# Chunked attention and two feed-forward networks: attention's steps placed one by one in the plan, a GpSimd subtraction cut into four

## The chip, the cores and the metric

The kernel runs on one core of one Trainium2 chip. The metric is the device time of one execution in microseconds. The engines work from queues of their own: TensorE (PE in the rows; PEld is its weight load), VectorE (DVE), ScalarE (ACT), GpSimd (POOL) and SyncE (SP), whose queue here only issues DMAs.

## The reference

Eight batches of eight heads with 576 positions of 64 features are cut into chunks of 64 positions, and each chunk attends to itself alone. The result, 4608 tokens of 512 features, goes through two feed-forward networks of width 2048.

```
scores = (q_c @ k_c^T) / 8;  scores -= max(scores)
attn   = exp(scores) / (sum(exp(scores)) + 1e-9)
x      = attn @ v_c                       # [4608, 512]
r = max(x @ w_in, 0);  y = (s * r*r + b) @ w_out
h = y @ w2_in;         out = (h * sigmoid(1.702 * h)) @ w2_out
```

## The kernel before

Tokens are worked on in nine blocks of 512 (j = 0 to 8). A product of fp32 accuracy is made of three TensorE matmuls, since every operand is kept as a high and a low part: low times high, high times high, high times low. The weights come as 64-bit floats and are decoded on the chip.

One product of the first network is `gemm_in(f, j, i)` (L511): 12 matmuls of 512 columns into a PSUM tile `h`. From it ScalarE makes `r` (ReLU, L531), VectorE `r = s * r * r` (L532), ScalarE the high part `gh` (L533) and VectorE the low part `gl` (L534). `gemm_out` (L579) then multiplies `gh` and `gl` with the second weights into four `acc` tiles (L594), also 12 matmuls. TensorE's order alternates the two, with `gemm_out` for index i two indices (`LAG`) behind `gemm_in`, so four products lie between the end of a product `h` and the first use of its `gh`. At the end of a block the `acc` tiles are copied out as `ost` (L602 on VectorE, L604 on ScalarE).

Attention of block j is done while the products of block j-1 run. A `Pair` (L236) is two heads of one block, four pairs to a block. Its generator `steps` (L301) is: `qt` and `kt` by two VectorE transposes of q and k (L272); 32 small score matmuls (L307); on VectorE the maximum (L316) and its subtraction (L317); the exponential on ScalarE (L322); on VectorE the sum (L324), 1e-9 (L325), the reciprocal (L326) and the product (L327) into `p`; `turn` (L276), eight VectorE transposes of 32 partitions by 256 columns (L281) into `pt`; `second` (L290), 32 small matmuls with v (L292); `split_x` (L297), the high and low parts of x. Blocks 0 and 1 use `EarlyPair`, whose transposes are TensorE's.

Beside this, from block 2 on, the second network's weights are decoded (`decode_second`, L175: a load into a `wst` tile, then L124 and L133 on ScalarE, L125, L128 and L134 on VectorE, L136 on GpSimd, and a DMA out from GpSimd's queue), and sums and differences of their quarters are made for a later stage of the Strassen kind (`sums`, L189). In `sums` everything is GpSimd's: four operations on 128 by 128 tiles (L198 to L201), a rounding to the high parts of seven such tiles at once (L203), the subtraction that leaves the low parts of the seven (L204, 896 columns), and two DMAs out (L209), the high parts first. The `wst` tiles are three: a decode holds one and a call of `sums` two.

After block 8 come `second_weights`, the first block of the second network, and the class `Halves`, which does the second network for pairs of blocks with seven products instead of eight.

The order is a plan written by hand. `at(t, f)` notes a function under a place t, `steps_at` notes the successive stretches of a generator, up to its next `yield`; at the end all notes are sorted by t and called, which traces the instructions. One unit of t is one product: `gemm_in` stands at 0.5 and `gemm_out` at 1.6 of every two units. The framework then sets the order of each engine's queue (`schedule_with_timeline_sim=True`): what was traced earlier has precedence among what its own time model takes to be ready. On the chip a queue is worked off in that order, and an instruction that waits holds what stands behind it. All short-lived tiles of [128, 512] (`qt`, `kt`, `p`, `pt`, `r`, `wm`, `wc`, `ost`) share ten places (`tmp`).

A pair is planned by these lines of `plan_attention` (L483), with o its base place; five notes for 13 stretches, so that four stretches (maximum to transposes) are traced together at o + 2:

```
at(o - 6.5, pr.load_qk)
at(o + 2.5, pr.load_v)
steps_at(((o - 2, 3), (o + 1, 1), (o + 2, 4), (o + 8, 1), (o + 8.5, 1)), pr.steps)
```

Of the kernel before, what the change touches and what calls it, by code (L numbers as in the profile page):

```python
# [8 lines left out]
F32 = mybir.dt.float32  # L9
F32R = mybir.dt.float32r  # L10
# [3 lines left out]
ALU = mybir.AluOpType  # L14
# [5 lines left out]
CH = 64  # L20
# [4 lines left out]


FIRST_STEPS = (0, 0.6, 0.8, 1.1, 1.8, 2.4, 2.7, 3.6, 3.9, 4.5)
LAG = 2
STAGED = 8
OPS = 4  # L30
# [16 lines left out]
def chunk_attention_two_ffn(ctx, tc, q, k, v, w1_in, w1_out, s, b, w2_in, w2_out, out):  # L47
# [6 lines left out]
    nc = tc.nc  # L54
# [49 lines left out]
    def tmp(name, dtype=F32):  # L104
        return tpool.tile([P, NB_MAX], dtype, tag="tmp", name=name)
# [38 lines left out]
    def staged():  # L144
        return stpool.tile([P, NB_MAX, 2], I32, tag="wst", name="wst")
# [43 lines left out]
    def sums(kind, i, z):  # L189

        q = staged().rearrange("p f z -> p (f z)").bitcast(F32).rearrange("p (t c) -> p t c", c=P)
        one, two = ((1, 2), (0, 3)) if kind == "wi" else ((1, 0), (2, 3))
        for t, (a, b) in ((i, one), (i + KF // 2, two)):
            for c, to in ((z, a), (2 + z, b)):
                nc.sync.dma_start(out=q[:, to, :], in_=w2_dram[kind][t][:, c * P:(c + 1) * P])
        yield
        a21, a11, a12, a22, s1, s2, s3, s4 = (q[:, t, :] for t in range(8))
        nc.gpsimd.tensor_tensor(out=s1, in0=a21, in1=a22, op=ALU.add)  # L198
        nc.gpsimd.tensor_tensor(out=s3, in0=a11, in1=a21, op=ALU.subtract)
        nc.gpsimd.tensor_tensor(out=s2, in0=s1, in1=a11, op=ALU.subtract)  # L200
        nc.gpsimd.tensor_tensor(out=s4, in0=a12, in1=s2, op=ALU.subtract)  # L201
        hi = staged().rearrange("p f z -> p (f z)").bitcast(F32R).rearrange("p (t c) -> p t c", c=P)[:, 0:7, :]
        nc.gpsimd.tensor_copy(out=hi, in_=q[:, 1:8, :])  # L203
        nc.gpsimd.tensor_tensor(  # L204
            out=q[:, 1:8, :].bitcast(F32R), in0=q[:, 1:8, :], in1=hi.bitcast(F32), op=ALU.subtract
        )
        to = wi_sums[i][:, :, z] if kind == "wi" else wo_sums[:, :, i, z]
        for part, src in enumerate((hi.bitcast(F32), q[:, 1:8, :])):
            nc.gpsimd.dma_start(out=to[:, :, part, :], in_=src)  # L209
# [15 lines left out]
    def quarters(nch):  # L225

        for i in range(nch // 2):
            for e in range(2):
                for h in range(2):
                    yield e, i, e * (nch // 2) + i, h, heads[h], heads[h ^ e]

    class Pair:  # L236
# [32 lines left out]
        def stage_qk(self):  # L269
            self.qt, self.kt = tmp("qt")[:, 0:self.n], tmp("kt")[:, 0:self.n]  # L270
            for t, src in ((self.qt, self.raw[0]), (self.kt, self.raw[1])):
                nc.vector.transpose(out=t.rearrange("p (u l) -> p u l", l=BK), in_=src)  # L272
            yield
            yield

        def turn(self, p):  # L276
            pt = tmp("pt")[:, 0:self.n].rearrange("p (c t) -> p c t", t=CH)
            for r in heads:
                for eq in range(2):
                    for ek in range(2):  # L280
                        nc.vector.transpose(  # L281
                            out=pt[r.start + ek * BK:r.start + (ek + 1) * BK, :, eq * BK:(eq + 1) * BK],
                            in_=p[r.start + eq * BK:r.start + (eq + 1) * BK, :, ek * BK:(ek + 1) * BK],
                        )
            return pt

        def room_scores(self):
            return left
# [12 lines left out]
        def steps(self):  # L301

            yield from self.stage_qk()
            yield
            ps = self.room_scores().rearrange("p e (c t) -> p e c t", t=CH)
            for e, i, c, h, r, other in quarters(self.nch):
                nc.tensor.matmul(  # L307
                    out=ps[other, e, i, :], lhsT=self.qt[r, c * CH:(c + 1) * CH], rhs=self.kt[r, c * CH:(c + 1) * CH],
                    start=True, stop=True,
                )  # L310
            yield
            mx = spool.tile([P, self.nch], F32, tag="mx", name="mx")
            sm = spool.tile([P, self.nch], F32, tag="sm", name="sm")
            p = tmp("p")[:, 0:self.n].rearrange("p (c t) -> p c t", t=CH)
            by_bank = mx.rearrange("p (e c) -> p e c", e=2)
            nc.vector.tensor_reduce(out=by_bank, in_=ps, axis=AX.X, op=ALU.max)  # L316
            nc.vector.tensor_tensor(  # L317
                out=p.rearrange("p (e c) t -> p e c t", e=2), in0=ps,
                in1=by_bank.unsqueeze(3).to_broadcast([P, 2, self.nch // 2, CH]), op=ALU.subtract,
            )  # L320
            yield
            nc.scalar.activation(out=p, in_=p, func=AF.Exp, scale=scale)  # L322
            yield
            nc.vector.tensor_reduce(out=sm, in_=p, axis=AX.X, op=ALU.add)  # L324
            nc.vector.tensor_scalar(out=sm, in0=sm, scalar1=1e-9, scalar2=None, op0=ALU.add)  # L325
            nc.vector.reciprocal(out=sm, in_=sm)  # L326
            nc.vector.tensor_tensor(  # L327
                out=p, in0=p, in1=sm.unsqueeze(2).to_broadcast([P, self.nch, CH]), op=ALU.mult
            )
            yield  # L330
            turned = self.turn(p)
            yield
            self.second(turned)
            yield
            self.split_x()
            done[0, self.j] = done.get((0, self.j), 0) + 1

    class EarlyPair(Pair):
# [21 lines left out]
        def turn(self, p):  # L360
            ps = acc_ps.tile([P, self.n], F32, tag=f"acc{2 * (self.hp % 2)}", name="pT")
            for i in range(self.n // P):
                nc.tensor.transpose(
                    ps[:, i * P:(i + 1) * P], p[:, 2 * i:2 * i + 2, :].rearrange("p c t -> p (c t)"), ident
                )
            pt = tmp("pt")[:, 0:self.n]
            nc.vector.tensor_copy(out=pt, in_=ps)
            return pt.rearrange("p (c h q) -> p c h q", h=2, q=CH)


        def room_scores(self):
# [92 lines left out]
    def at(t, f, *a):  # L464
        ITEMS.append((t, len(ITEMS), f, a))

    def steps_at(times, make, after_x=False):

        st = {}

        def step(n):
            g = st.setdefault("g", make())
            traced = nc.cur_bb.bb.instructions
            old = len(traced)
            for _ in range(n):
                next(g, None)
            for ins in traced[old:] if after_x else ():
                if ins.engine in first_x:
                    tc.add_manual_dep(ins, first_x[ins.engine].name, IN_ORDER, reason="behind the first x")
        for t, n in times:  # L480
            at(t, step, n)

    def plan_attention(j):  # L483

        base = NS * (j - 1)
        for p in range(HP):
            pr, o = Pair(j, p), base + (-6 + 8 * p if j == 2 else 7 * p - 3)
            at(o - 6.5, pr.load_qk)
            at(o + 2.5, pr.load_v)
            steps_at(((o - 2, 3), (o + 1, 1), (o + 2, 4), (o + 8, 1), (o + 8.5, 1)), pr.steps)  # L490

    def plan_y(j):
        base = NS * (NBLK + j - 1)
# [349 lines left out]
    def plan_first_blocks():  # L843
        for j in range(2):
# [8 lines left out]
            for p in range(HP):  # L853
                pr = EarlyPair(early, p)
                o = FIRST + (3 + 4 * p if j else -13 + 1.9 * p)
                steps_at([(o + t, 1) for t in FIRST_STEPS], pr.steps, after_x=j == 1)

# [40 lines left out]
    for j in range(2, NBLK):  # L898
        plan_attention(j)
    plan_y(0)  # L900
    for n, (i, kind) in enumerate((i, kind) for i in range(KF // 2) for kind in ("wi", "wo")):
        t = 2 * NS + -2.0 + 13.3 * n
        steps_at(((t, 1), (t + 2.0, 1)), lambda kind=kind, i=i: decode_second(kind, i))
        steps_at(((t + 4, 1), (t + 4 + 2.0, 1)), lambda kind=kind, i=i: decode_second(kind, i + KF // 2))
        steps_at(((t + 10, 1), (t + 10 + 2.0, 1)), lambda kind=kind, i=i: sums(kind, i, 0))
        steps_at(((t + 13, 1), (t + 13 + 2.0, 1)), lambda kind=kind, i=i: sums(kind, i, 1))
# [6 lines left out]
    for z in range(2, NBLK + 1):  # L913
        f, j = divmod(z, NBLK)
        for i in range(KF):
            at(NS * z + 2 * i + 0.5, first_product, f, j, i)
            at(NS * z + 2 * (i + LAG) + 1.6, lambda *a: gemm_out(*a, G.pop(a)), f, j, i)
    for p in range(NBLK // 2):
        Halves(1 + 2 * p, NS * (NBLK + 1) + 2 * LAG + 56 * p).plan()
    traced, last = nc.cur_bb.bb.instructions, None  # L920
# [32 lines left out]
```

## Time and profile before

| | |
|---|---|
| time, median of 3 runs | 1676.16 us (1675.64 to 1676.69) |
| the profiled execution's own time | 1671.44 us |
| its span, first to last instruction | 1669.6 us |
| TensorE busy | 1592.9 us, 95% of the span |
| VectorE busy | 1183.2 us, 71% |
| ScalarE busy | 720.6 us, 43% |
| GpSimd busy | 364.9 us, 22% |
| mean granted TensorE clock | 0.977 |
| L281, VectorE transposes of `p` | 224 instructions, 97.7 us busy |
| L204, GpSimd's low parts | 32 instructions, 74.3 us busy |

The busy share is of the whole span. [...] In a row of the timeline the brackets hold the idle time of that engine just before the instruction, and what ended it.

### The profile page before, as it was taken

The numbers are of one execution on the slowest core, as the hardware profiler recorded it, in microseconds if no ns is written. First come the engines' busy times: TensorE is split into PE (matmuls) and PEld (weight loads), VectorE is DVE, ScalarE is ACT, GpSimd is POOL, SyncE is SP. The second block draws the span as 40 slices with busy tenths as digits, with TensorE's granted clock in tenths as the row PEclk, the third lists the DMA queues.
The fourth block names the chain that finished last, engine by engine and source line by source line (L and its number), as shares of the span: only waits on it lengthen the run. The fifth ranks groups of instructions, "written<-read, shape, count | busy, mean of one in ns | idle before, by whom it ended". The sixth has DMA issues, their size and how long they took to land.

```text
span 1669.6 us, 24650 instructions
## 1 busy us (share of the span) xinstructions
PE 1592.9 (95%) x8928; PEld 1293.2 (77%) x8928; DVE 1183.2 (71%) x1832; ACT 720.6 (43%) x1222; POOL 364.9 (22%) x390
## 2 busy tenths in 40 slices
PE   5889999999999999899999999999999999999998
PEld 4668877787877788678888888888887888788876
DVE  5786757878766787777866644469667956894685
ACT  3668634323322333223334533446345534553552
POOL 1322101444444434344454210000000000100000
PEclk8889999999999999899999999999999999999999
DMA  9425444545455454545337551576767686768663
GB/s 231 110 101 149 129 130 124 149 136 152 124 145 137 120 151 126 149 127 151 103 118 223 167 161 35 182 227 228 201 210 251 195 224 204 243 180 239 209 202 76
DMA packets 348937, 272.19 MB, mean 163 GB/s; under 512 B 256144, under 2 KB 288912, under 8 KB 348816
## 3 DMA queue, kind: packets, MB, share of 16 engines
q1 hardware_dynamic: 333200, 220.28, 47.3%
q0 software_dynamic: 13312, 46.15, 8.3%
q10 hardware_dynamic: 2304, 4.20, 0.7%
q8 instruction: 70, 1.15, 0.3%
q14 instruction: 51, 0.42, 0.1%
HBM read 209.72 MB, written 60.82 MB: 162 GB/s over the span
## 4 chain that ended last, share of the span: by engine, by line
PE 51%; DVE 1%; ACT 0%; issue 0%; ACTq 0%
PE x L789 10%; PE x L694 10%; PE acc L594 7%; PE h L519 7%; PE at L694 5%; PE at L789 5%; PE b L694 3%; PE b L789 3%; DVE wo L716 0%; DVE pt L281 0%; ACT r L715 0%; PE at L292 0%; PE at L307 0%; DVE p L327 0%; DVE gl L534 0%
## 5 line engine op out<-in xcount | busy, mean ns | idle before, releaser
L519 PE MATMUL h<-xh,wi 128*128 128x512 f32 x1280 | 404.5, 398 | 10.0 <-ACT r L549 8.6
L594 PE MATMUL acc<-gh,wo 128*128 128x512 f32 x1152 | 363.0, 403 | 15.3 <-ACT gh L533 8.8
L519 PEld LDWEIGHTS h<-xh,wi 128*128 128x128 f32 x1280 | 242.3, 191 | 63.8 <-ACT r L549 10.1
L594 PEld LDWEIGHTS acc<-gh,wo 128*128 128x128 f32 x1152 | 220.8, 194 | 65.1 <-ACT gh L533 10.6
L519 PE MATMUL h<-xl,wi 128*128 128x512 f32 x640 | 251.9, 394 | 0.0
L594 PE MATMUL acc<-gl,wo 128*128 128x512 f32 x576 | 225.4, 402 | 12.3 <-DVE gl L534 12.2
L533 ACT ACTIVATE gh<-r,sb 128x512 fp32r<-128x512 f32 x112 | 80.9, 723 | 235.0 <-DVE r L532 234.7
L534 DVE SCALAR_TENSOR_TENSOR gl<-r,sb,gh 128x512 fp32r<-128x512 f32 x112 | 113.2, 1012 | 50.7 <-ACT gh L533 50.7
L594 PEld LDWEIGHTS acc<-gl,wo 128*128 128x128 f32 x576 | 111.3, 193 | 40.6 <-DVE gl L534 17.1
L519 PEld LDWEIGHTS h<-xl,wi 128*128 128x128 f32 x640 | 122.1, 191 | 26.2
L630 POOL DMA_DIRECT2D xr<-y x32 | 17.6, 549 | 506.7 <-ACT r L715 242.4
L532 DVE SCALAR_TENSOR_TENSOR r<-r,sb 128x512 f32<-128x512 f32 x112 | 109.0, 976 | 21.8 <-ACT r L531 21.3
L136 POOL TENSOR_TENSOR wm<-wm,wc 128x512 int32<-128x512 int32 x52 | 77.8, 1498 | 211.1 <-DVE wm L134 140.4
L716 DVE TENSOR_TENSOR wo<-wo,r 128x512 f32<-128x512 f32 x96 | 66.1, 692 | 74.4 <-ACT r L715 74.0
L766 ACT ACTIVATE op<-wo 128x512 fp32r<-128x512 f32 x128 | 80.1, 631 | 79.3 <-PE x L789 28.2
L789 PE MATMUL x<-op,wi 128*128 128x512 f32 x432 | 105.1, 389 | 0.0
L281 DVE STREAM_TRANSPOSE pt<-p 32x256 f32<-32x256 f32 x224 | 97.7, 436 | 4.1
L531 ACT ACTIVATE r<-h 128x512 f32<-128x512 f32 x112 | 65.8, 587 | 77.7 <-PE h L519 69.4
L694 PE MATMUL x<-xh,wi 128*128 128x512 f32 x320 | 99.0, 389 | 0.0
L715 ACT ACTIVATE r<-wo 128x512 f32<-128x512 f32 x96 | 60.8, 633 | 88.2 <-DVE wo L713 87.4
L767 DVE TENSOR_TENSOR op<-wo,op 128x512 fp32r<-128x512 f32 x128 | 86.0, 680 | 11.8 <-ACT op L766 10.4
L789 PEld LDWEIGHTS x<-op,wi 128*128 128x128 f32 x432 | 81.1, 188 | 16.8
(149 smaller groups left out, 2786.5 us busy)
## 6 DMA issues: line engine op xcount, KB each, us to landing
wi<-wo_sums SPq DMA_DIRECT2D x112, 512.0 KB, 3.8
wi<-wi_sums SPq DMA_DIRECT2D x96, 512.0 KB, 3.6
wst<-in_moe_w_out SPq DMA_DIRECT2D x32, 512.0 KB, 3.8
wi_sums<-wst POOLq DMA_DIRECT2D x32, 448.0 KB, 4.3
wo_sums<-wst POOLq DMA_DIRECT2D x32, 448.0 KB, 4.2
wst<-in_moe_w_in SPq DMA_DIRECT2D x24, 512.0 KB, 4.2
y<-ost SPq DMA_DIRECT2D x36, 256.0 KB, 3.2
xr<-y POOLq DMA_DIRECT2D x32, 256.0 KB, 4.4
```

Of the source, the lines that this page charges most:

```text
L136: nc.gpsimd.tensor_tensor(out=t, in0=t, in1=c.bitcast(I32), op=ALU.add)
L281: nc.vector.transpose(out=pt[r.start + ek * BK:r.start + (ek + 1) * BK, :, eq * BK:(eq + 1) * BK], in_=p[r.start + eq * BK:r.start + (eq + ...
L519: nc.tensor.matmul(out=ps, lhsT=w_[:, kk, :], rhs=x_, start=kk == 0 and a == 0, stop=kk == KD - 1 and a == 2,)
L532: nc.vector.scalar_tensor_tensor(out=r, in0=r, scalar=s_ap, in1=r, op0=ALU.mult, op1=ALU.mult)
L533: nc.scalar.activation(out=gh, in_=r, func=AF.Identity, bias=b_ap)
L534: nc.vector.scalar_tensor_tensor(out=gl, in0=r, scalar=b_ap, in1=gh.bitcast(F32), op0=ALU.add, op1=ALU.subtract)
L594: nc.tensor.matmul(out=acc[m], lhsT=l_, rhs=r_, start=i == 0 and a == 0, stop=i == KF - 1 and a == 2)
L694: nc.tensor.matmul(out=self.ps[key], lhsT=l_, rhs=r_, start=start and k == 0 and a == 0, stop=k == HK - 1 and a == 2, skip_group_check=not ...
L716: nc.vector.tensor_tensor(out=g, in0=h, in1=r, op=ALU.mult)
L766: nc.scalar.activation(out=hi, in_=src, func=AF.Copy)
L767: nc.vector.tensor_tensor(out=lo, in0=src, in1=hi.bitcast(F32), op=ALU.subtract)
L789: nc.tensor.matmul(out=self.ps[key], lhsT=l_, rhs=r_, start=start and i == 0 and a == 0, stop=i == HF - 1 and a == 2, skip_group_check=not ...
```

## The change

`PAIR_STEPS` gives 13 places, one for each stretch of `Pair.steps`. The two transposes of q and k are now at o - 2 and o - 1.5 (the third place, o - 1, has nothing in it); the score matmuls stay at o + 1; the maximum and its subtraction go from o + 2 to o + 1.9, the exponential to o + 2.2, sum to product to o + 3, and the eight transposes, two at a time, to o + 3.7, 4.2, 4.7 and 5.2. `second` and `split_x` stay at o + 8 and o + 8.5. No note that issues a DMA is moved. `EarlyPair` is adapted to the new form of `turn` and does the same at the same places. In `sums`, the subtraction L204 over seven tiles becomes four, over two, two, two and one (256, 256, 256 and 128 columns); both DMAs stay behind all four.

```
--- before.py
+++ after.py
@@ -25,6 +25,7 @@
 
 
 FIRST_STEPS = (0, 0.6, 0.8, 1.1, 1.8, 2.4, 2.7, 3.6, 3.9, 4.5)
+PAIR_STEPS = (-2, -1.5, -1, 1, 1.9, 2.2, 3, 3.7, 4.2, 4.7, 5.2, 8, 8.5)
 LAG = 2
 STAGED = 8
 OPS = 4
@@ -201,9 +202,12 @@
         nc.gpsimd.tensor_tensor(out=s4, in0=a12, in1=s2, op=ALU.subtract)
         hi = staged().rearrange("p f z -> p (f z)").bitcast(F32R).rearrange("p (t c) -> p t c", c=P)[:, 0:7, :]
         nc.gpsimd.tensor_copy(out=hi, in_=q[:, 1:8, :])
-        nc.gpsimd.tensor_tensor(
-            out=q[:, 1:8, :].bitcast(F32R), in0=q[:, 1:8, :], in1=hi.bitcast(F32), op=ALU.subtract
-        )
+
+        for t0, t1 in ((0, 2), (2, 4), (4, 6), (6, 7)):
+            nc.gpsimd.tensor_tensor(
+                out=q[:, 1 + t0:1 + t1, :].bitcast(F32R), in0=q[:, 1 + t0:1 + t1, :], in1=hi[:, t0:t1, :].bitcast(F32),
+                op=ALU.subtract,
+            )
         to = wi_sums[i][:, :, z] if kind == "wi" else wo_sums[:, :, i, z]
         for part, src in enumerate((hi.bitcast(F32), q[:, 1:8, :])):
             nc.gpsimd.dma_start(out=to[:, :, part, :], in_=src)
@@ -270,11 +274,11 @@
             self.qt, self.kt = tmp("qt")[:, 0:self.n], tmp("kt")[:, 0:self.n]
             for t, src in ((self.qt, self.raw[0]), (self.kt, self.raw[1])):
                 nc.vector.transpose(out=t.rearrange("p (u l) -> p u l", l=BK), in_=src)
-            yield
-            yield
+                yield
 
         def turn(self, p):
-            pt = tmp("pt")[:, 0:self.n].rearrange("p (c t) -> p c t", t=CH)
+
+            self.pt = pt = tmp("pt")[:, 0:self.n].rearrange("p (c t) -> p c t", t=CH)
             for r in heads:
                 for eq in range(2):
                     for ek in range(2):
@@ -282,7 +286,7 @@
                             out=pt[r.start + ek * BK:r.start + (ek + 1) * BK, :, eq * BK:(eq + 1) * BK],
                             in_=p[r.start + eq * BK:r.start + (eq + 1) * BK, :, ek * BK:(ek + 1) * BK],
                         )
-            return pt
+                    yield
 
         def room_scores(self):
             return left
@@ -328,9 +332,8 @@
                 out=p, in0=p, in1=sm.unsqueeze(2).to_broadcast([P, self.nch, CH]), op=ALU.mult
             )
             yield
-            turned = self.turn(p)
-            yield
-            self.second(turned)
+            yield from self.turn(p)
+            self.second(self.pt)
             yield
             self.split_x()
             done[0, self.j] = done.get((0, self.j), 0) + 1
@@ -365,7 +368,8 @@
                 )
             pt = tmp("pt")[:, 0:self.n]
             nc.vector.tensor_copy(out=pt, in_=ps)
-            return pt.rearrange("p (c h q) -> p c h q", h=2, q=CH)
+            self.pt = pt.rearrange("p (c h q) -> p c h q", h=2, q=CH)
+            yield
 
 
         def room_scores(self):
@@ -487,7 +491,8 @@
             pr, o = Pair(j, p), base + (-6 + 8 * p if j == 2 else 7 * p - 3)
             at(o - 6.5, pr.load_qk)
             at(o + 2.5, pr.load_v)
-            steps_at(((o - 2, 3), (o + 1, 1), (o + 2, 4), (o + 8, 1), (o + 8.5, 1)), pr.steps)
+
+            steps_at([(o + t, 1) for t in PAIR_STEPS], pr.steps)
 
     def plan_y(j):
         base = NS * (NBLK + j - 1)
```

## Rows read from the trace of the kernel before

**Rows 1.** Windows, two stretches: length; busy PE, PEld, DVE, ACT, POOL; clock; DMA.

```profile
284.00:810.00 526.00, 501.32 (x3390) 402.69 (x3389) 398.84 (x606) 162.21 (x266) 236.12 (x254) 0.97 0.52 138
...
810.00:1669.60 859.60, 846.74 (x3814) 698.20 (x3812) 587.04 (x898) 394.86 (x673) 78.75 (x96) 1.00 0.61 186
```

**Rows 2.** Waits of TensorE between 284 and 810 us: us in total, times, longest.

```profile
PE acc L594 <- DVE gl L534: 12.2, 7, 2.6
PE acc L594 <- ACT gh L533: 8.8, 3, 4.6
PE acc L594 <- ACT ost L604: 2.0, 2, 1.3
PE acc L594 <- DVE ost L602: 1.6, 2, 0.8
```

**Rows 3.** Windows view of three 20 us slices, columns as in rows 1.

```profile
480.00:500.00 20.00, 18.23 (x67) 14.57 (x68) 13.79 (x25) 5.70 (x10) 4.92 (x6) 0.83 0.53 165
...
520.00:540.00 20.00, 17.74 (x129) 13.93 (x128) 12.46 (x15) 6.13 (x10) 10.39 (x10) 0.91 0.65 170
...
1280.00:1300.00 20.00, 18.53 (x83) 14.99 (x82) 18.00 (x30) 13.95 (x24) 1.09 (x2) 1.00 0.76 254
```

**Rows 4.** Timeline near 396 us: start, us, engine, line, operation [idle before <-releaser].

```profile
393.79 0.43 DVE L125 TENSOR_SCALAR wm<-wst 128x512 int32<-128x512 int32 x1 [1.63 <-DMA wst<-in_moe_w_out]
...
396.35 2.39 POOL L204 TENSOR_TENSOR wst<-wst 128x896 fp32r<-128x896 f32 x1
...
396.74 2.55 DVE L534 SCALAR_TENSOR_TENSOR gl<-r,sb,gh 128x512 fp32r<-128x512 f32 x1
...
399.34 0.51 PE L594 MATMUL acc<-gl,wo 128*128 128x512 f32 x1 [2.55 <-DVE gl L534]
```

**Rows 5.** Timeline near 700 us.

```profile
696.11 0.58 ACT L531 ACTIVATE r<-h 128x512 f32<-128x512 f32 x1
...
697.40 2.34 DVE L327 TENSOR_TENSOR p<-p,sm 128x512 f32<-128x512 f32 x1
...
699.77 3.58 DVE L281 STREAM_TRANSPOSE pt<-p 32x256 f32<-32x256 f32 x8
...
703.39 0.75 DVE L532 SCALAR_TENSOR_TENSOR r<-r,sb 128x512 f32<-128x512 f32 x1
...
704.95 1.22 PE L594 MATMUL acc<-gh,wo 128*128 128x512 f32 x2 [4.61 <-ACT gh L533]
```

**Rows 6.** Timeline near 325 us.

```profile
324.80 0.80 PE L594 MATMUL acc<-gl,wo 128*128 128x512 f32 x1 [2.09 <-DVE gl L534]
```

**Rows 7.** Timeline near 465 us.

```profile
464.20 3.60 DVE L281 STREAM_TRANSPOSE pt<-p 32x256 f32<-32x256 f32 x8
...
465.51 2.12 POOL L204 TENSOR_TENSOR wst<-wst 128x896 fp32r<-128x896 f32 x1
```

**Rows 8.** Timeline near 550 us.

```profile
549.10 0.46 POOL L199 TENSOR_TENSOR wst<-wst 128x128 f32<-128x128 f32 x1
...
549.13 0.97 DVE L534 SCALAR_TENSOR_TENSOR gl<-r,sb,gh 128x512 fp32r<-128x512 f32 x1 [0.79 <-ACT gh L533]
...
549.51 0.90 POOL L198 TENSOR_TENSOR wst<-wst 128x128 f32<-128x128 f32 x1
...
550.02 0.94 DVE L532 SCALAR_TENSOR_TENSOR r<-r,sb 128x512 f32<-128x512 f32 x1
```

**Rows 9.** Groups of instructions between 284 and 810 us: xcount, busy, mean ns, idle.

```profile
L204 POOL TENSOR_TENSOR wst<-wst 128x896 fp32r<-128x896 f32 x25 | 57.4, 2296 | 1.0
...
L316 DVE TENSOR_REDUCE mx<-at 128x8 f32<-128x512 f32 x21 | 14.3, 679 | 0.4 <-PE at L307 0.4
```

**Rows 10.** Waits of VectorE between 284 and 810 us.

```profile
DVE wm L125 <- DMA wst<-in_moe_w_in: 33.6, 7, 7.6
DVE wm L125 <- DMA wst<-in_moe_w_out: 21.8, 5, 6.1
```

**Rows 11.** Chain that ended last, just after 810 us: start, us, what.

```profile
812.06 2.72 PE acc L594 x12
```

More of the change, by code (lines that the diff above doesn't have):

```diff
@@ L27 @@
 FIRST_STEPS = (0, 0.6, 0.8, 1.1, 1.8, 2.4, 2.7, 3.6, 3.9, 4.5)
+PAIR_STEPS = (-2, -1.5, -1, 1, 1.9, 2.2, 3, 3.7, 4.2, 4.7, 5.2, 8, 8.5)
 LAG = 2
@@ L203, in sums @@
         nc.gpsimd.tensor_copy(out=hi, in_=q[:, 1:8, :])
-        nc.gpsimd.tensor_tensor(
-            out=q[:, 1:8, :].bitcast(F32R), in0=q[:, 1:8, :], in1=hi.bitcast(F32), op=ALU.subtract
-        )
+        for t0, t1 in ((0, 2), (2, 4), (4, 6), (6, 7)):
+            nc.gpsimd.tensor_tensor(
+                out=q[:, 1 + t0:1 + t1, :].bitcast(F32R), in0=q[:, 1 + t0:1 + t1, :], in1=hi[:, t0:t1, :].bitcast(F32),
+                op=ALU.subtract,
+            )
         to = wi_sums[i][:, :, z] if kind == "wi" else wo_sums[:, :, i, z]
@@ L272, in stage_qk @@
                 nc.vector.transpose(out=t.rearrange("p (u l) -> p u l", l=BK), in_=src)
-            yield
-            yield
+                yield
         def turn(self, p):
-            pt = tmp("pt")[:, 0:self.n].rearrange("p (c t) -> p c t", t=CH)
+            self.pt = pt = tmp("pt")[:, 0:self.n].rearrange("p (c t) -> p c t", t=CH)
             for r in heads:
@@ L284, in turn @@
                         )
-            return pt
+                    yield
         def room_scores(self):
@@ L330, in steps @@
             yield
-            turned = self.turn(p)
-            yield
-            self.second(turned)
+            yield from self.turn(p)
+            self.second(self.pt)
             yield
@@ L367, in turn @@
             nc.vector.tensor_copy(out=pt, in_=ps)
-            return pt.rearrange("p (c h q) -> p c h q", h=2, q=CH)
+            self.pt = pt.rearrange("p (c h q) -> p c h q", h=2, q=CH)
+            yield
         def room_scores(self):
@@ L489, in plan_attention @@
             at(o + 2.5, pr.load_v)
-            steps_at(((o - 2, 3), (o + 1, 1), (o + 2, 4), (o + 8, 1), (o + 8.5, 1)), pr.steps)
+            steps_at([(o + t, 1) for t in PAIR_STEPS], pr.steps)
     def plan_y(j):
```

## The prediction

> **What bounds the kernel now.** I read the windows view first, to see where TensorE loses time. The reader is to see that it loses nothing worth naming after 810 us (busy 846.7 of 859.6 us, clock 1.00; the rest is four gaps of about 1.47 us and the last copies out), and 24.7 us between 284 and 810 us, at a mean clock of 0.97 [rows 1]. That stretch is the products of blocks 2 to 7 with the pairs and the weight work beside them; up to 284 us the kernel lives on its first loads and on the first weights, and there are only four of the changed pairs and none of the calls of `sums`.
>
> Next the waits of TensorE in the stretch: 24.6 us, all before L594; for `gl` 12.2 us in seven gaps, for `gh` 8.8 in three, for `ost` 3.6 in four [rows 2]. So no product waits for attention's result; products wait for their own `gh` and `gl`, which are late on VectorE.
>
> Then the clock, slice by slice. A gap of about 2 us or more is followed by a time at half speed: the slice with the gap near 529 us has a mean of 0.91, the one with several gaps near 480 us 0.83, and a slice that held a 1.47 us gap alone kept 1.00 [rows 3]. Of the 20 us slices between 320 and 760 us, six stand at 0.91 or 0.92 and two at 0.83; times 20 us this is 6 x 1.7 + 2 x 3.4 = 17 us. With the gaps, the stretch loses 24.6 + 17 = about 42 us. No edit here can win more there.
>
> Last the timeline around each gap, to see what VectorE did. There are three kinds.
> *Holds.* L204 runs on GpSimd from 396.35 for 2.39 us; `gl` of a product, started on VectorE 0.39 us later, lasts 2.55 us and ends 0.55 us after L204 does, where an instruction of this kind takes 0.75 alone (L532 in [rows 5]); TensorE waits 2.55 us [rows 4]. The same picture stands at 481, 529 and 694 us, with gaps of 1.91, 2.25 and 2.33: four gaps, 9.0 us. In each, `gl` was already late, since VectorE had stood at L125 for a `wst` load [rows 4].
> *Bursts.* `r` is ready for VectorE at 696.69, but the sum, the product and eight transposes of a pair stand ahead of it, and it starts at 703.39; TensorE waits 4.61 us [rows 5]. Two more bursts end in gaps of 2.59 (549 us) and 1.62 us (750 us): with 0.27 and 0.78 for the `gl` behind two of them, 9.9 us.
> *The rest.* 2.09 us for a `gl` behind a late load alone [rows 6], and the 3.6 us for `ost` at block ends.
>
> **The change, part by part.**
> *Places of the pair's steps.* No instruction and no DMA is added or taken away, and no load is moved; on TensorE's queue nothing is moved either. What changes is who has precedence on VectorE. One unit of the plan is one product, 2.72 us [rows 11]. From the sum (o + 3) to the last transposes (o + 5.2) the pair's 5.4 us of work now have two or three notes of products between them, and a `gemm_in` at o + 2.5 comes ahead of the sum, so its `r` and `gl` pass. At 697 us `r` would have run 6 us sooner. At 549 and 750 us I take the whole gaps back (2.59 + 0.27 + 1.62 + 0.78 = 5.3 us); at 705 us 3.6 of 4.61, since the pair's product there was itself held 1.65 us by a GpSimd instruction [rows 5], which `r` may meet instead. That is 8.9 us. Their slices' clocks, two at 0.91 and one at 0.83, cost 1.8 + 1.8 + 3.4 = 7.0 us, which go with the gaps. Sum of the bursts: 15.9 us. The cover for the transposes being later: they end by plan 2.8 units, 7.6 us, before the matmuls that read `pt`. Moving the transpose of k by half a unit is worth nothing: it has two units before the scores.
> The transposes don't touch GpSimd's conflict: eight of them last 3.60 us with an L204 of 2.12 beside them, neither longer than alone [rows 7].
>
> *L204 in four.* The price of a piece: 128 columns take 0.46 us [rows 8], 896 take 2.12 [rows 7]; on the line between, 256 columns take 0.74, so the four take 3 x 0.74 + 0.46 = 2.68 us, 0.56 more. If each later piece waits for a VectorE instruction, it is up to 0.44 more for each (0.90 beside 0.46 [rows 8]), so at most about 1.9 us more in all. The lower bound is 0 (the cuts cost nothing); I take 0.56. GpSimd is 45% busy in the stretch, 236 of 526 us [rows 1], so its own queue hides 25 x 0.56 = 14 us [rows 9]; but the DMAs (L209) stand behind the four pieces, the `wst` places come free behind these DMAs, and the loads that L125 waits for behind those. So each such wait grows by about 0.56 us.
> What a held instruction gains: it waits for one piece of 0.74 in place of the whole 2.12, 1.38 us. Four holds: 5.5 us, less 4 x 0.56 = 2.2 for the later loads, 3.3 us. Their gaps come to about 1.5 us, near the one that left the clock alone [rows 3], so I count the clock of three slices back (1.7 each) and half of that at 480 us: 6.9 us. Sum of the holds: 10.2 us. The two bounds are 0 (gaps remain long enough for the clock) and 9.0 + 8.6 = 17.6.
>
> Does a held instruction get in between the pieces? Four rows say so: `gl` waits for L199 and ends at 550.10; L198, started at 549.51, takes 0.90; then comes `r` on VectorE, until 550.96 [rows 8]. They alternate, one instruction each.
> [...]
>
> *The gap at 325 us* grows by 0.56 us. *New gaps.* The order of the queue is made anew around all of this; four holds and three bursts in 21 pairs and 25 L204s [rows 9] were coincidences of this order, and another has its own. I take three gaps of 1.2 us and one slice at 0.91: 3.6 + 1.8 = 5.4 us.
>
> The sum: 15.9 + 10.2 - 0.6 - 5.4 = 20.1 us. The profiled execution's own time is 1671.4 us, so 1651.3; the median of the runs is 4.7 us above it, so **1656 us**. After 810 us nothing takes it back: TensorE runs without a wait there, and what it needs then comes from the same queues as now.
>
> **The rivals.**
> *A. Only the places pay.* The holds' gain is eaten, because `gl`, `r` and the decode's instructions are caught by one piece after the other and the clock still falls. For it: a gap near 1.5 us lies close to those that cost the clock. Against: one instruction of 0.74 per piece lets the late `gl`, which is first, go. 15.9 - 0.6 - 5.4 - 1.4 (holds no better, loads later) = 8.5 gained: 1668.
> [...]
> *C. The loads become the bound: slower.* VectorE already stands at L125 twelve times in the stretch, 55.4 us in all, up to 7.6 [rows 10], and five of these waits end in a gap. If every piece meets a VectorE instruction, each wait grows by 1.9 us; if all twelve then end in a gap, that costs 12 x 1.9 = 23 us, and seven new falls of the clock 7 x 1.7 = 12, against 15.9 from the bursts and 3 from the holds: 16 slower, 1692. Working it back, it decides from a growth of about 0.6 us when all seven others also end in a gap that costs the clock, and not at all while they keep their slack. For it: 0.56 is the price without any meeting. Against: seven waits of 4 us on average passed without a gap.
> *D. The pair gets late: no change.* `p` keeps its place among the ten for longer, from o + 1.9 to o + 5.2, beyond the next pair's allocation at o + 5, and `pt` is finished later. If TensorE waits 1 us for each of the stretch's 21 pairs, at L292 or for a place for `r`, the gain is gone: 1676. Against: 7.6 us of cover, and no wait of TensorE before L292 or L307 in the stretch now [rows 2].
>
> **How the numbers follow.** Forecast 0.57, A 0.18, B 0.04, C 0.13, D 0.08. From no change a measurement can tell about 0.2%, 3.4 us. Faster: forecast, A and B, less 0.02 of A's low end: 0.77. Same: D and that, 0.10. Slower: C, 0.13. The forecast's own range goes from both terms in full with half of the new gaps (15.9 + 17.6 - 0.6 - 2.7 = 30 gained, 1646) to the bursts with a third of the holds (12 gained, 1664). For 8 in 10 it is drawn to 1642, for the 42 us that are there to be won, and up to 1676, over A, B and D.
>
> **What the new profile would show.** Right: between 284 us and the end of block 7, waits of TensorE below 13 us, none for `gh` over 1.5 us, the mean clock at 0.98 or above; `gl` never over 1.6 us; four L204 of 0.46 to 1.2 us; VectorE's transposes in twos with `r` or `gl` between. Wrong by C: waits at L125 well over 55 us with a gap behind most. Wrong by D: TensorE waits before L292 or L307, or ScalarE before L531 for a tile. [...]

## The result, and the profile after

The changed kernel takes 1695.16 us (median of four, 1693.52 to 1696.94) beside 1675.90 us (1670.28 to 1676.69) for the kernel before: a ratio of 1.0122 [1.0098, 1.0147], 19.3 us slower. The profiled executions lie 25.5 us apart (1696.94 and 1671.44), since that of before fell 4.5 us under its median and this one 1.8 us above.

The windows, columns as in [rows 1]. The first stretch is drawn to 828 us, where the kernel has done as many matmuls as before at 810 (3385 and 3390).

```profile
284.00:828.00 544.00, 505.82 (x3385) 402.14 (x3384) 378.33 (x611) 163.43 (x267) 259.83 (x328) 0.97 0.50 132
828.00:1695.20 867.20, 849.83 (x3814) 699.01 (x3812) 579.08 (x897) 393.38 (x671) 89.83 (x119) 1.00 0.63 185
```

The same work takes 18.0 us more. TensorE is busy 4.5 us more at the same mean clock of 0.97; the rest is waits. (The clock is the share of TensorE's full speed that the profile lists as granted. Around the gap of 2.25 us near 529 us of the kernel before it is 1.00 from 520 to 529 us, 0.50 from 529.5 to 532.5 and 1.00 from 533 to 540.) VectorE is busy 20.5 us less than in [rows 1], so it gained what the change was meant to give it. GpSimd is busy 23.7 us more.

The waits of TensorE from 284 to 828 us, columns as in [rows 2].

```profile
PE acc L599 <- DVE gl L539: 11.6, 11, 2.9
PE acc L599 <- ACT gh L538: 9.5, 8, 2.6
PE acc L599 <- DVE ost L607: 5.9, 4, 3.2
PE at L296 <- DVE pt L285: 5.6, 5, 2.3
PE h L524 <- ACT r L536: 4.2, 3, 2.0
PE at L311 <- DVE kt L276: 0.7, 1, 0.7
PE acc L599 <- ACT ost L609: 0.4, 1, 0.4
```

They come to 37.9 us, 13.3 more than the 24.6 of before. No gap is as long as the 4.6 us of [rows 2], but there are more of them, for nearly everything that VectorE and ScalarE make. A further 4.4 us of such waits lie between 828 and 960 us, where the kernel before has none. What VectorE waited for, same stretch, against [rows 10]:

```profile
DVE wm L126 <- DMA wst<-in_moe_w_in: 54.8, 9, 12.0
DVE wm L126 <- DMA wst<-in_moe_w_out: 38.5, 8, 8.0
```

L126 is L125 of before, VectorE's first instruction of a decode. It stands 93.3 us in 17 waits, where it stood 55.4 in twelve. The groups of GpSimd there (busy, mean ns, idle before):

```profile
L207 POOL TENSOR_TENSOR wst<-wst 128x256 fp32r<-128x256 f32 x75 | 71.1, 974 | 1.0
L213 POOL DMA_DIRECT2D wi_sums<-wst x25 | 22.6, 904 | 37.0 <-issue 34.0 <-DVE wm L129 3.0
L213 POOL DMA_DIRECT2D wo_sums<-wst x24 | 21.6, 901 | 33.7 <-issue 31.2 <-DMA vs<-in_v 2.5
L207 POOL TENSOR_TENSOR wst<-wst 128x128 fp32r<-128x128 f32 x25 | 16.7, 669 | 0.0
```

The four pieces take 3 x 0.974 + 0.669 = 3.59 us a call, the whole took 2.30 [rows 9]: 1.29 us more, not 0.56. Four pieces took 2.78 us at 396.51 us, where VectorE stood idle, and 3.75 at 480.89, where instructions of VectorE of 1.05 to 1.27 us stood beside them. The place of [rows 4] in the timeline now:

```profile
396.51 2.78 POOL L207 TENSOR_TENSOR wst<-wst 128x256 fp32r<-128x256 f32 x4
...
398.55 0.67 ACT L125 ACTIVATE wc<-wst 128x512 int32<-128x512 uint32 x1 [8.64 <-DMA wst<-in_moe_w_out]
398.55 0.43 DVE L126 TENSOR_SCALAR wm<-wst 128x512 int32<-128x512 int32 x1 [5.88 <-DMA wst<-in_moe_w_out]
399.01 0.88 DVE L285 STREAM_TRANSPOSE pt<-p 32x256 f32<-32x256 f32 x2
...
399.93 0.75 DVE L537 SCALAR_TENSOR_TENSOR r<-r,sb 128x512 f32<-128x512 f32 x1
...
401.48 0.73 PE L599 MATMUL acc<-gh,wo 128*128 128x512 f32 x2 [2.59 <-ACT gh L538]
...
403.49 0.80 PE L599 MATMUL acc<-gl,wo 128*128 128x512 f32 x1 [1.27 <-DVE gl L539]
```

No instruction of VectorE is held here: `r` takes 0.75 us. But it stands behind L126, which waits 5.88 us for its load, and TensorE still loses 2.59 + 1.27 us. What the load waits for is to be seen in the chain that ended last, at 600 us (start, us, what):

```profile
602.50 1.98 DMA wst<-w_wo
604.55 0.46 POOL wst L199
...
606.12 2.25 POOL wst L207 x3
608.36 3.58 DMA wo_sums<-wst
612.07 4.28 DMA wst<-in_moe_w_in
616.43 0.69 ACT wc L125
...
619.75 3.85 DMA wst<-in_moe_w_in
623.62 1.39 DVE wm L126
625.02 0.66 DVE r L537
```

This is a loop through the three `wst` tiles: a call of `sums` gets its quarters, GpSimd works on them, the DMA out lands, only then is the tile free and the next load starts, and only then can the decode go on, with `r` behind it. The loop was there before the change. Between 284 and 960 us of the kernel before, SyncE's queue, which issues the loads, stands 108.3 us before decodes' loads (L112 and L118) for a DMA out of `sums`:

```profile
SPq L118 <- DMA wi_sums<-wst: 55.2, 10, 12.9
SPq L112 <- DMA wo_sums<-wst: 53.1, 10, 12.1
```

It stands another 97.5 us before loads of quarters (L195) for the DMA out of a decode, which closes the loop through the decode. And two rows of GpSimd's timeline show a part of the loop in which the profile has no work, between the two DMAs of one call:

```profile
484.59 0.89 POOL L213 DMA_DIRECT2D wi_sums<-wst  x1
491.20 0.90 POOL L213 DMA_DIRECT2D wi_sums<-wst  x1 [5.73 <-issue]
```

The change did not bring this part: in the whole run such waits before the DMAs of `sums` come to 84.8 us, and to 86.5 in the kernel before.

The page's chain by engine, before PE 51% and DVE 1%, with nothing named of loads or `sums`, is now

```profile
PE 59%; DVE 10%; DMA 9%; POOL 7%; issue 6%; SPq 5%; ACT 2%; POOLq 0%; DVEq 0%; ACTq 0%
```

### The profile page after: what moved, and what is told of

The parts are those of the page before. It is cut to its first block, busy times and chain, and to the rows that moved or that the text cites. A ratio compares the mean times of both kernels' runs of the same rounds, so it can differ in the third digit from the quotient of the medians.

```text
span 1695.2 us, 24741 instructions
## 1 busy us (share of the span) xinstructions
PE 1598.5 (94%) x8928; PEld 1292.2 (76%) x8928; DVE 1150.4 (68%) x1832; ACT 719.9 (42%) x1222; POOL 398.9 (24%) x486
## 4 chain that ended last, share of the span: by engine, by line
PE 59%; DVE 10%; DMA 9%; POOL 7%; issue 6%; SPq 5%; ACT 2%; POOLq 0%; DVEq 0%; ACTq 0%
PE acc L599 12%; PE x L794 10%; PE x L699 10%; PE h L524 10%; PE at L699 5%; PE at L794 5%; POOL wst L207 3%; PE b L794 3%; PE b L699 3%; SPq L256 2%; DMA wo_sums<-wst 2%; DMA wi_sums<-wst 2%; DVE r L537 1%; DVE pt L285 1%; DMA wst<-in_moe_w_in 1%
## 5 line engine op out<-in xcount | busy, mean ns | idle before, releaser
L524 PE MATMUL h<-xh,wi 128*128 128x512 f32 x1280 | 405.1, 398 | 14.8 <-ACT r L554 9.1
L539 DVE SCALAR_TENSOR_TENSOR gl<-r,sb,gh 128x512 fp32r<-128x512 f32 x112 | 102.2, 914 | 44.4 <-ACT gh L538 44.1
L137 POOL TENSOR_TENSOR wm<-wm,wc 128x512 int32<-128x512 int32 x52 | 75.1, 1446 | 192.0 <-DVE wm L135 170.6
L207 POOL TENSOR_TENSOR wst<-wst 128x256 fp32r<-128x256 f32 (+1 forms) x128 | 112.9, 911 | 1.4
L537 DVE SCALAR_TENSOR_TENSOR r<-r,sb 128x512 f32<-128x512 f32 x112 | 96.2, 860 | 23.2 <-ACT r L536 22.5
L126 DVE TENSOR_SCALAR wm<-wst 128x512 int32<-128x512 int32 x52 | 24.8, 483 | 113.9 <-DMA wst<-in_moe_w_in 64.1
```

Source lines behind the costliest of these rows:

```text
L137: nc.gpsimd.tensor_tensor(out=t, in0=t, in1=c.bitcast(I32), op=ALU.add)
L207: nc.gpsimd.tensor_tensor(out=q[:, 1 + t0:1 + t1, :].bitcast(F32R), in0=q[:, 1 + t0:1 + t1, :], in1=hi[:, t0:t1, :].bitcast(F32), op=ALU.s ...
L524: nc.tensor.matmul(out=ps, lhsT=w_[:, kk, :], rhs=x_, start=kk == 0 and a == 0, stop=kk == KD - 1 and a == 2,)
L537: nc.vector.scalar_tensor_tensor(out=r, in0=r, scalar=s_ap, in1=r, op0=ALU.mult, op1=ALU.mult)
L539: nc.vector.scalar_tensor_tensor(out=gl, in0=r, scalar=b_ap, in1=gh.bitcast(F32), op0=ALU.add, op1=ALU.subtract)
```

## The experiments

The theory after the result (called L or R in the expectations): the loop paces blocks 2 to 8, and what lengthens a call of `sums` ahead of its DMAs is paid for, since it isn't hidden by GpSimd's idle time. Against it: the places do it (P); the queues' order fell out badly, by accident (Q); VectorE's own order and holds set the gaps, whatever the loads do (V); it is the cutting itself, not the length (W). Every kernel was timed against the kernel before on the same chip.

**The two halves, and a measure of accident.** Kernel e1 is the changed kernel with the whole subtraction (first edit); e2 is the kernel before with the cut alone (second):

```
-        for t0, t1 in ((0, 2), (2, 4), (4, 6), (6, 7)):
...
+        nc.gpsimd.tensor_tensor(
+            out=q[:, 1:8, :].bitcast(F32R), in0=q[:, 1:8, :], in1=hi.bitcast(F32), op=ALU.subtract
+        )
```

```
-        nc.gpsimd.tensor_tensor(out=q[:, 1:8, :].bitcast(F32R), in0=q[:, 1:8, :], in1=hi.bitcast(F32), op=ALU.subtract)
+        for u, w in ((0, 2), (2, 4), (4, 6), (6, 7)):
+            lo = q[:, 1 + u:1 + w, :]
+            nc.gpsimd.tensor_tensor(out=lo.bitcast(F32R), in0=lo, in1=hi[:, u:w, :].bitcast(F32), op=ALU.subtract)
```

> Only the 13 places, the subtraction stays one instruction of 896 columns. Theory L (the cut subtraction makes the loads of wst late, VectorE and ScalarE stand longer for them): the places alone are 8 to 16 us faster than before (1660 to 1668), VectorE's waits at the decode's first instruction stay near the 62 us of before over blocks 2 to 8. Theory P (the places themselves do it: the pair is late, or the decode's waiting instruction now stands ahead of a product's): 10 to 20 us slower than before (1686 to 1696), with TensorE waiting before the pair's matmuls. Theory Q (the order of the queues is made anew by any edit and the sum of its accidents moves by some 10 us either way): anywhere from 1665 to 1690.

> Only the cut of the subtraction into four, all the places as before. Theory L: 10 to 20 us slower than before (1686 to 1696), VectorE's waits for wst loads near the 110 us of the changed kernel. Theory P: 0 to 10 us faster (1666 to 1676), no gap before gl over 1.5 us. Theory Q: 1665 to 1690, not the sum's remainder of the other run.

e1: 1676.09, ratio 1.0008 [0.9992, 1.0024]. e2: 1694.78, 1.0123 [1.0101, 1.0145]. The cut alone makes the whole loss, so P falls. But the places alone are worth nothing, which the theory had not expected either: in e1, too, VectorE waits for loads more than before (83.2 us in eighteen between 284 and 960 us, where it was 62.5 in fourteen). e2 in the same stretch:

```profile
DVE wm L125 <- DMA wst<-in_moe_w_in: 62.5, 10, 11.8
DVE wm L125 <- DMA wst<-in_moe_w_out: 38.3, 7, 8.6
```

e4 is the kernel before with decodes and `sums` planned 0.4 of a unit later, for what a new order alone can do:

```
-        t = 2 * NS + -2.0 + 13.3 * n
+        t = 2 * NS + -1.6 + 13.3 * n
```

> The kernel before with all decodes and sums planned 0.4 unit (1.1 us) later: no instruction is added or moved against its neighbours of the same helper. Theories L and P: within 4 us of before. Theory Q: 5 us or more away from it in either direction, by other gaps at other places.

1681.39, 1.0029 [1.0010, 1.0048]. In this one trial an accident of order, or the later start of the loads, is worth 5.6 us by the medians: just over the border of 5 us that was set for Q, and a quarter of the loss. So a difference of 5 us between two kernels here proves nothing. Q does not reach to e2, which lies outside its range of 1665 to 1690 and has the loss of the change.

**The DMA of the high parts first.** The high parts are ready after the rounding. If their DMA goes out ahead of the subtraction, one of the call's two tiles comes free earlier, and the cut can't delay it. e3 is this in the changed kernel, e5 in the kernel before; e6 is e5 with the cut, e7 is e5 with the places. The left-out lines are the subtraction, whole or in four.

```
+        nc.gpsimd.dma_start(out=to[:, :, 0, :], in_=hi.bitcast(F32))
...
-        for part, src in enumerate((hi.bitcast(F32), q[:, 1:8, :])):
-            nc.gpsimd.dma_start(out=to[:, :, part, :], in_=src)
+        nc.gpsimd.dma_start(out=to[:, :, 1, :], in_=q[:, 1:8, :])
```

> Both parts of the change, but the DMA of the high parts is issued before the four subtractions, which shortens the time that a call of sums holds its two wst tiles by 2.5 to 4 us. Theory L: most of the loss is gone, 1670 to 1680, waits for wst loads below 80 us. Theories P and Q: within 8 us of the changed kernel (1687 to 1703) or moved without a change of these waits.

> The kernel before with one edit: the DMA of the high parts is issued ahead of the subtraction, which stays whole; places as before. Theory R (over blocks 2 to 8 the three wst tiles are the bound: a call of sums holds two of them from the load to the landing of its DMAs, and whatever lengthens or shortens that moves the end): 15 to 25 us faster than before (1651 to 1661), the last low parts landed 20 us sooner. Theory V (VectorE's order and its holds set the gaps, the loads only move them): within 5 us of before.

> High parts' DMA first and the cut into four, places as before. Theory R: with the ring of tiles slack, the cut costs little; against the run with the whole subtraction 3 us faster to 5 us slower. Theory V: the cut costs its 19 us here too (1690 or more).

> High parts' DMA first and the 13 places, the subtraction whole. Theory R: the places now pay, since products are no longer held by loads: 5 to 12 us faster than with the DMA alone (1643 to 1654). Theory V: the places are worth as little as without the DMA's move, within 3 us of the run with the DMA alone.

| kernel | DMA first and | median, us | ratio |
|---|---|---|---|
| e5 | nothing else | 1653.82 | 0.9885 [0.9870, 0.9899] |
| e6 | the cut | 1650.15 | 0.9861 [0.9846, 0.9876] |
| e7 | the places | 1643.51 | 0.9824 [0.9809, 0.9839] |
| e3 | both, the change | 1646.52 | 0.9831 [0.9800, 0.9861] |

Moving one DMA issue gains 20 us in the kernel before and 49 in the changed one, without an instruction less; in the changed one that is far more than was expected. V, which allowed 5 us to e5, falls. The waits for loads collapse; in e5 between 284 and 960 us (62.5 us of them in the kernel before, 100.8 in e2):

```profile
DVE wm L125 <- DMA wst<-in_moe_w_in: 10.6, 6, 4.7
DVE wm L125 <- DMA wst<-in_moe_w_out: 10.0, 3, 5.6
```

The edit does two things. The high parts' tile comes free earlier, and the subtraction now stands where GpSimd waited between the two DMAs: the "issue" waits before the DMAs of `sums` come to 14.8 us in e5, where the kernel before has 86.5. Which of the two is worth more these runs don't tell.

With the loop slack, the places are worth the 10 us that they weren't in e1 (e5 to e7; TensorE's waits for `gh` fall from 9.1 to 0.2 us). The cut costs nothing that can be told from accident: 3.7 us less from e5 to e6, and from e7 to e3, on different chips, a ratio of 0.9831 after 0.9824.

**Length or cutting.** e9 leaves the subtraction whole and puts a delay at the same place in the kernel before: four of the seven high parts are rounded twice more. e8 puts a delay ahead of the rounding: the first addition (L198) is done three times.

```
         nc.gpsimd.tensor_copy(out=hi, in_=q[:, 1:8, :])
+        for _ in range(2): nc.gpsimd.tensor_copy(out=hi[:, 0:4, :], in_=q[:, 1:5, :])
```
```
-        nc.gpsimd.tensor_tensor(out=s1, in0=a21, in1=a22, op=ALU.add)
+        for _ in range(3): nc.gpsimd.tensor_tensor(out=s1, in0=a21, in1=a22, op=ALU.add)
```

> The kernel before with the first addition of each call of sums done three times over (the same values written again), 0.9 us more of GpSimd's time in short instructions ahead of the DMAs; nothing is cut, no place is moved. Theory R: 8 to 18 us slower than before (1684 to 1694), by the length alone. Theory V: 0 to 4 us slower, since the added instructions are short and hold little.

> The kernel before with four of the seven high parts rounded twice more (the same values), about 1.2 us more of GpSimd's time between the first rounding and the DMAs, where the cut adds its time; the subtraction stays whole and the places stay. Theory R: 12 to 22 us slower than before (1686 to 1698), as with the cut, since the length counts and not the cutting. A theory W, that the cut pieces do it by catching VectorE and being caught more often: within 8 us of before (up to 1682).

e9: 1697.60, 1.0120 [1.0105, 1.0135]. Its groups on GpSimd between 284 and 960 us, and the waits of VectorE there:

```profile
L204 POOL CAST wst<-wst 128x512 fp32r<-128x512 f32 x64 | 50.8, 794 | 1.6
```
```profile
DVE wm L125 <- DMA wst<-in_moe_w_out: 54.9, 11, 9.7
DVE wm L125 <- DMA wst<-in_moe_w_in: 36.3, 10, 6.5
```

2 x 0.794 = 1.59 us more a call with no cut anywhere, and the loss is that of the change; VectorE's busy time, 1184.5 us, is close to the 1183.2 of the kernel before. W falls. e8 lost less than expected: 1680.54, 1.0045 [1.0028, 1.0061], 6.6 us for a GpSimd that is busy 34.2 us more, 1.07 us a call. That is below the 8 us of R and above the 4 of V. The row of the rounding in the kernel before (284 to 960 us) shows where part of it went:

```profile
L203 POOL CAST wst<-wst 128x896 fp32r<-128x896 f32 x32 | 34.9, 1092 | 58.8 <-DMA wi_sums<-wst 31.5 <-DMA wo_sums<-wst 26.2
```

The rounding needs a tile of its own and stands 58.8 us for DMAs of earlier calls that still hold one. In e8 this wait is 43.0 us, 15.8 less: a delay ahead of the rounding partly vanishes in it. In e9, with the delay behind the rounding, it is 65.3. Whether that is the whole difference, or an accident of order as in e4 adds to it, these runs don't tell apart.

**A fourth tile.** e10 is the changed kernel with four `wst` tiles, paid for with one of the ten `tmp` places:

```
-    tpool = ctx.enter_context(tc.tile_pool(name="tpool", bufs=10))
-    stpool = ctx.enter_context(tc.tile_pool(name="stpool", bufs=3))
+    tpool = ctx.enter_context(tc.tile_pool(name="tpool", bufs=9))
+    stpool = ctx.enter_context(tc.tile_pool(name="stpool", bufs=4))
```

> The changed kernel with four wst tiles in place of three; the room for it comes from one of the ten short-lived tiles, which can only hurt. Theory R: the loads no longer wait for a call of sums, 1645 to 1665, VectorE's waits for wst loads below 50 us. Theory W or V: 1690 or more.

1671.90, 0.9965 [0.9953, 0.9976]: less than expected, but by the ratios some 26 us better than the change, with the cut in it. GpSimd's rounding hardly waits for a tile any more (2.1 us between 284 and 960 us). Of the waits for loads one row is left between 284 and 960 us; three rows of TensorE's waits there:

```profile
DVE wm L126 <- DMA wst<-in_moe_w_in: 4.5, 3, 3.0
```
```profile
PE acc L599 <- ACT gh L538: 7.5, 2, 4.8
PE acc L599 <- DVE ost L607: 6.0, 1, 6.0
PE acc L599 <- DVE gl L539: 2.5, 3, 1.2
```

The two long gaps that remain come from the shortage among nine `tmp` places. VectorE's waits in the same stretch show it; the first ends at 675.57 us and the gap of 4.8 at 678.19, the longer part of the second (10.9) at 475.77 and the gap of 6.0 at 476.52:

```profile
DVE wm L126 <- DMA y<-ost: 15.9, 1, 15.9
DVE ost L607 <- POOL wm L137: 11.5, 2, 10.9
```

`wm` and `ost` are among the tiles that share these places. In the kernel before the only such wait there is one of 2.6 us.

**Another queue.** e11 is e7 with both DMAs of `sums` issued from SyncE's queue; e12 is that with the cut.

```
-        nc.gpsimd.dma_start(out=to[:, :, 0, :], in_=hi.bitcast(F32))
+        nc.sync.dma_start(out=to[:, :, 0, :], in_=hi.bitcast(F32))
...
-        nc.gpsimd.dma_start(out=to[:, :, 1, :], in_=lo)
+        nc.sync.dma_start(out=to[:, :, 1, :], in_=lo)
```

> High parts' DMA first, places new, subtraction whole, and both DMAs of sums issued from SyncE's queue in place of GpSimd's. Theory R: the second DMA no longer follows the first by more than 4 us on GpSimd, the tiles come free sooner, 3 to 10 us faster than with GpSimd's queue (1634 to 1641), unless SyncE's queue, which then waits for GpSimd ahead of other loads, gives it back (1650 or more).

> Both parts of the change, the high parts' DMA first and both DMAs from SyncE's queue: the run before with the cut added. Theory R: with the wst tiles coming free early the cut costs and gives little, 1624 to 1634. If the cut's added GpSimd time still stands in the ring's way, 1636 or more; if the shorter holds are worth something once the loads are out of the way, below 1624.

e11: **1627.77 us, 0.9708 [0.9692, 0.9724]**, 50 us under the kernel before on its chip and the best here. It is also better than expected. e12: 1633.05, 0.9753 [0.9721, 0.9784]; by the ratios the cut takes some 7 us back, though the intervals just touch, and VectorE's waits for loads are 50.8 us in it. In e11 the windows view and TensorE's waits up to 960 us have the stretch almost without loss:

```profile
284.00:828.00 544.00, 542.33 (x3732) 442.71 (x3731) 416.83 (x674) 185.94 (x300) 217.81 (x232) 1.00 0.57 146
```
```profile
PE acc L599 <- DVE gl L539: 1.3, 1, 1.3
PE acc L599 <- ACT gh L538: 0.3, 1, 0.3
```

In the same 544 us it does 3732 matmuls, the changed kernel 3385. VectorE still waits 23.5 us for loads (14.3 in seven and 9.2 in three), but only 1.6 us of TensorE's time is lost. SyncE's queue waits 7.3 us before decodes' loads for the DMAs of `sums`, where it was 108.3. The step from e7 to e11 has a second part that isn't told apart from this one: VectorE is held less (busy 1202.1 us in e7, 1150.5 in e11; longest `gl` 4.78 and 2.58).

Over the runs the end of the loop and the time go together. The last rounding of `sums` starts at 957.0 us in e9, 955.7 in the changed kernel, 955.2 in e2, 939.2 in e8, 927.4 in the kernel before, 902.1 in e5 and 874.2 in e11, which is also the order of what they gained or lost. e10 is off this line (909.4), with its gaps for `tmp`.

## Why the prediction was wrong

I gave 0.77 to faster and forecast 1656 us; rival C, at 0.13 and 1692 us, is what came. (The low end of the forecast's own range, "12 gained", comes to 13.3 by its own terms; nothing hangs on it.)

*The step that failed* is the pricing of the cut: "I take 0.56", and then "its own queue hides 25 x 0.56 = 14 us", with 2.2 us taken off the holds and 0.6 for one gap. The size was off by a factor of two: 1.29 us a call. Its 2.68 us for four pieces is near the 2.78 at 396.51, where they met no instruction of VectorE. The bound of 1.9 us from the pieces that meet a VectorE instruction [rows 8] held the measured value, and I took the other end. But e9 and e5 show that the hiding was the worse error. GpSimd has idle time, as I read from [rows 1]; that time is not slack. In the kernel before, 255 of its 379 us between 284 and 960 us are waits inside the loop: 111 for quarters (L198, L199), 58 for a tile to round into (L203) and 86 between the two DMAs. Much of a delay behind the rounding runs round the loop instead of into GpSimd's idle time: 25 calls of 1.29 us are 32 us, and the stretch is 18 us longer. Where the other 14 us were hidden is not shown. How much of a delay is paid for differs: 32 calls of 1.59 us cost 19.5 us in e9, 32 of 1.07 cost 6.6 in e8.

*Reading gaps by what ended last* failed with it. Each of the holds and bursts was real, and I counted 26 us for them, but `gl` "was already late" behind a load in all four holds, as the prediction itself says. The late load was the cause that recurs, the hold what came on top. Where a hold goes, the next late load finds another instruction to be late. I asked what each gap needed and not what paced the waits of L125, though [rows 10] had 55.4 us of them.

*The holds* (10.2 us): in the changed kernel VectorE was held less, as I had said. Its busy time fell from 1183.2 to 1150.4 us in the whole run, and between 284 and 828 us `gl` is never longer than 1.80 us (source view of L539, where [rows 4] has 2.55; one of 2.26 follows at 880 us, beside a DMA issue of GpSimd):

```profile
L539 DVE SCALAR_TENSOR_TENSOR gl<-r,sb,gh x86: 708/752/1796, 282.3 to 825.6; 128x512 fp32r<-128x512 f32 x86
```

It bought no time: the cut alone (e2) has the same fall, to 1148.2, and the whole loss. Nor does the term appear where the loop is slack: the 3.7 us from e5 to e6 are within accident, and VectorE's busy time does not fall there (1189.1 and 1198.7).

*Rival B*, put at 0.04, was a `gl` that lasts over all four pieces; no row of the kernel before had shown that. For this stretch of the changed kernel the same row refutes it: the longest `gl` takes 1.80 us. In e6 its picture is found, behind the issue of the first DMA (713.51 us): the four pieces run without a break, in 2.66 us, and a `gl` of 3.65 us beside them ends only after the last.

```profile
714.30 2.66 POOL L208 TENSOR_TENSOR wst<-wst 128x256 fp32r<-128x256 f32 x4
715.11 3.65 DVE L534 SCALAR_TENSOR_TENSOR gl<-r,sb,gh 128x512 fp32r<-128x512 f32 x1 [0.79 <-ACT gh L533]
```

So that a held instruction gets in between the pieces, which the prediction took from [rows 8], holds in the changed kernel, where at 480.89 us two instructions of VectorE that last 1.05 and 1.22 us end at 481.36 and 482.50 and the next pieces start at 481.92 and 483.05, and does not hold in e6. What decides it no run here shows.

*The bursts* (15.9 us): right about VectorE, wrong about the time. Alone (e1) the places gain nothing, in a loop with slack (e5 to e7) 10.3 us, two thirds of the term. *Rival A*, only the places pay, thereby falls as well. *Rival D* came in part: TensorE waits 5.6 us before L296 for `pt`, in e1 4.5, where 7.6 us of cover were counted; with the loop slack 1.3 (e7) and 2.5 (e3) are left. *New gaps* (5.4 us): the 5.6 us of e4 are of that size, in a single trial.

*Rival C* had the right mechanism and sign of proof ("waits at L125 well over 55 us": 93.3). Its price was built from the wrong part, each existing wait growing by 1.9 us. Measured, the growth is 1.29 a call, there are five more waits of the kind, and the clock cost little: TensorE's busy time in the stretch grew by 4.5 us, where I had put 12. That its sum came near is luck: it has 35 us of loss less 19 for the bursts and the holds, where the cut alone lost 19 and the places alone gained nothing.

## What to carry to other kernels

An engine that is idle half the time can still be in the loop that sets the pace, as GpSimd is here (busy 260 of 544 us in the changed kernel): before an added instruction is booked as hidden, follow the buffer that it holds to the next load, and count how many times in the run that loop goes round. When most gaps begin with the same late load, ask what makes that load late before what ended each gap: in e5 VectorE's waits for loads fell from 62.5 to 20.6 us and the time by 20. Here it paid to issue a DMA out straight behind the instruction that makes its data (e5), and from SyncE's queue in place of GpSimd's (e7 to e11, ratios 0.9824 and 0.9708, with VectorE held less as well). Ask of every added delay where on the path it stands: a microsecond behind the rounding (e9, 19.5 us for 1.59 a call) cost about twice as much as one ahead of it (e8, 6.6 us for 1.07).

## What the runs showed of the hardware

The pieces of the subtraction on GpSimd took 0.974 us for 256 columns and 0.669 for 128 on average between 284 and 828 us of the changed kernel, against 2.30 us for 896 in one between 284 and 810 us of the kernel before. The four together took 2.78 us beside an idle VectorE (396.51) and 3.75 with instructions of VectorE of 1.05 to 1.27 us beside them (480.89).

With a DMA issue on GpSimd directly ahead of the subtraction, an instruction of VectorE lasted over more than one of GpSimd's in e7: `gl` lasted 4.78 us from 703.49, while GpSimd issued the DMA (703.42), subtracted (704.21, 2.26 us) and went on to L137 (706.27). In the kernel before, the longest `gl` is 2.61.

Two DMAs of 448 KB issued one after the other from GpSimd's queue stood apart by an "issue" wait of up to 5.73 us, 34.0 + 31.2 us in all over the 49 issues of the groups above; what causes this wait no run here shows. With both on SyncE's queue (e11) GpSimd has no such wait, and the time to landing is 3.6 us. The page of e11, DMA issues (KB each, us to landing), where the changed kernel has 4.1 and 4.0:

```profile
wi_sums<-wst SPq DMA_DIRECT2D x32, 448.0 KB, 3.6
wo_sums<-wst SPq DMA_DIRECT2D x32, 448.0 KB, 3.6
```
